# A sequence transform moved ahead of a gated MLP, with every MLP block in seven products

## The chip, the cores and the metric

The kernel runs on one core of one Trainium2 chip. The metric is device microseconds of one execution of the program. One execution on the chip is also profiled, and all rows below come from that one. Engines are named as the profile names them: PE (TensorE, matrix products; PEld is its weight load), DVE (VectorE), ACT (ScalarE), POOL (GpSimd) and SP (SyncE, which here only issues DMAs).

## The reference

`x` is 2048 tokens by 512 features. `xn` is its layernorm without affine terms. The first branch takes a discrete Fourier transform along the features and then along the tokens and keeps the real part. The second is an MLP with a sigmoid gate and 1792 hidden features. The output joins them.

```python
xn = (x - mean(x)) / sqrt(var(x) + 1e-5)
a, b = xn @ Wd_re.T, xn @ Wd_im.T            # 512 x 512 matrices
s = Ws_re @ a - Ws_im @ b                    # 2048 x 2048 matrices
h = sigmoid(xn @ w_gate) * (xn @ w_up)       # 512 x 1792 each
out = x + s * silu(h @ w_down)               # 1792 x 512
```

Both transforms are linear, so the sequence matrices can be applied to `xn` first and the feature matrices last. Both kernels do that.

## The kernel before

**Products.** Every value enters a product as two parts: `hi`, a copy rounded to fp32r that ACT writes, and `lo`, the rest, which DVE gets by a subtraction. `mm3` (lines 74 to 77) makes one product of three matmuls: hi by hi, hi by lo, lo by hi. A matmul has a weight of 128 by 128 and 512 moving columns, unless said otherwise. `Parts` makes the pair from a raw tile: one ACT instruction (line 71), then one DVE instruction (line 72).

**Seven products.** A block of two by two sub-blocks is multiplied by seven products in place of eight (Strassen's scheme in Winograd's form). The sums and differences that it needs are DVE instructions of `combine` (line 123). The products are numbered 1 to 7 and add up in chains "a", "b" and "c", each in two of the eight PSUM banks: ga and ua, gb and ub, gc and uc, or the two called pd. ACT snaps a chain's state between two products.

**Stages.** First the MLP: `BLOCKS` lists pairs (h, g), h being one of two halves of the tokens and g one of seven groups of 256 hidden features. Block (0, 0) is special (`start`, the local function `begin`): x arrives by tokens, is normalised on DVE, turned by 32 PE transposes (line 215), and multiplied in 192 matmuls of 256 columns (line 543) as the turned pieces come in. The other thirteen blocks compute gate and up by seven products (84 matmuls). Their down product is a `Seven` of 42 matmuls or, for group 2 in half 0, a `Plain` of 48; block (0, 0) has a `Ready` of 48. Each down product's result goes by `gather`: ACT evicts two banks into a page (line 309), POOL issues a DMA that adds the page onto `g_part` in DRAM (line 311). The second half's tokens are normalised while the first half's blocks run: DVE statistics, POOL arithmetic on the moments (lines 165 to 171), ACT normalisation (line 176), and a DMA of the result to `xn_part`. The same tokens are also needed as features by tokens; they are loaded so from `x_t` and normalised on DVE with moments broadcast from `m_part`.

Then the sequence transform (`seq_units`): four chunks of 512 output tokens, each 28 units of 12 matmuls. A unit is one product k for one pair of token blocks pp. Its weights are parts of normalised x, read back from `xn_part` and `s_part` and kept through all four chunks; its moving operand is a sum of blocks of the two cosine and sine matrices. Results and their sums go to `f_part`. Last the feature transform (`hidden_units`), 28 units of 12 matmuls, whose result is multiplied by silu of `g_part` (made ahead, stored in `gs_part`) and added onto the output by a DMA, the output having been filled with x.

**Order.** The kernel is recorded unit by unit, and each engine runs its instructions in the order recorded. For unit n the loop at the end of the kernel first runs what `sooner` put at n, then issues the loads of units n to n+5, then makes the parts of units n to n+2, then records the matmuls, then what `after` put at n. All buffers of SBUF are 54 pages of 4 KB per partition; a new page takes the place of one whose last use lies back, and the engine that writes it first waits for that use to end, a DMA's landing included. POOL's queue carries the moment arithmetic and the issues of all stores and adding DMAs; SP's carries all loads.

Of the kernel before, what the change touches and what calls it, by code (L numbers as in the profile page):

```python
# [36 lines left out]
def fnet_glu_kernel(ctx: ExitStack, tc: tile.TileContext, x, x_t, c_re, c_im, w_h, w_gu, w_down, out):  # L37
# [15 lines left out]
    ident = const.tile([P, P], F32, name="ident")  # L53
    make_identity(nc, ident)
    ones = const.tile([P, 512], F32R, name="ones")
    nc.vector.memset(ones.bitcast(F32), 1.0)
    mhalf = const.tile([P, 1], F32, name="mhalf")
    nc.gpsimd.memset(mhalf, -0.5)
    warm = const.tile([P, 1], F32, name="warm")
    nc.scalar.activation(warm, mhalf, AF.Sigmoid)  # L60
    moments = const.tile([P, 3, KH], F32, name="moments")
    m_part = dram.tile([2, 2, SB], F32, name="m_part")
    xn_part = dram.tile([2, 2, 2, P, 4, D // 2], F32, name="xn_part")
    g_part = [dram.tile([P, 2, SB], F32, name=f"g_part{i}") for i in range(2 * NT)]
    gs_part = dram.tile([2 * NT, P, 2, SB], F32, name="gs_part")
    f_part = dram.tile([NT // 2, 2, 7, P, 2, SB], F32, name="f_part")
    w_part = dram.tile([4, P, 4, D // 2], F32, name="w_part")
    s_part = dram.tile([2, 4, P, 4, D // 2], F32, name="s_part")
# [5 lines left out]
    def mm3(ps, ws, ms, first, last, go_on=False):  # L74
        nc.tensor.matmul(ps, ws[0], ms[0], start=first, stop=False, skip_group_check=go_on)  # L75
        nc.tensor.matmul(ps, ws[0], ms[1], start=False, stop=False, skip_group_check=go_on)  # L76
        nc.tensor.matmul(ps, ws[1], ms[0], start=False, stop=last, skip_group_check=go_on)  # L77
# [28 lines left out]
    class Parts(Value):  # L106


        def __init__(self, loads, src, shape, joint=False):
            def make():  # L110
                s = src()
                if joint:
                    both = page([2, *shape])
                    hi, lo = both[:, 0], both[:, 1]
                else:
                    hi, lo = page(shape), page(shape)
                split(hi, lo, s)
                return hi, lo

            super().__init__(loads, make)  # L120
# [5 lines left out]
    XK = {(0, 0): 1, (1, 0): 2, (0, 1): 0, (1, 1): 3}  # L126
    xop = {}
    xraw = {}
# [5 lines left out]
    extra, early = {}, {}  # L134
    now = [0]
# [6 lines left out]


    xs = {}

    def fetch(i, hold=False):
        pg = page([2, D], F32)
        if hold:
            nc.vector.memset(pg[:, 0, :1], 0.0)
        for j in range(2):  # L150
            xs[i + j] = pg[:, j, :]
            nc.sync.dma_start(xs[i + j], x[(i + j) * P : (i + j + 1) * P, :])

    st_of = {}

    def norm_a(i):
        st = stat.tile([P, 6], F32, name="st")
        mv = stat.tile([P, 2], F32, name="mv")
        rs = stat.tile([P, 2], F32, name="rs")
        nc.vector.bn_stats(st, xs[i])  # L160
        nc.vector.bn_aggr(mv, st)
        mean, scale = mv[:, 0:1], rs[:, 1:2]
        if i >= KH:
            mean, scale = (moments[:, m, i - KH : i - KH + 1] for m in range(2))
            nc.gpsimd.tensor_scalar(mean, mv[:, 0:1], 0.0, None, op0=ALU.add)
        nc.gpsimd.tensor_scalar(rs[:, 0:1], mv[:, 1:2], EPS, None, op0=ALU.add)
        nc.gpsimd.tensor_tensor(scale, rs[:, 0:1], mhalf, op=ALU.pow)
        if i >= KH:
            bias = moments[:, 2, i - KH : i - KH + 1]
            nc.gpsimd.tensor_tensor(bias, mean, scale, op=ALU.mult)  # L170
            nc.gpsimd.tensor_scalar(bias, bias, -1.0, None, op0=ALU.mult)
        st_of[i] = mean, scale

    def second_norm(i):
        scale, bias = (moments[:, m, i - KH : i - KH + 1] for m in (1, 2))
        nc.scalar.activation(xs[i], xs[i], AF.Identity, scale=scale, bias=bias)

    def norm_b(i):
        mean, scale = st_of.pop(i)
        nc.vector.tensor_scalar(xs[i], xs[i], mean, scale, op0=ALU.subtract, op1=ALU.mult)  # L180

    def turned_half(n, b, at):

        both = Load(m_part[b].rearrange("m t -> (m t)").partition_broadcast(P).rearrange("p (m t) -> p m t", m=2), [2, SB])
        raw = [Load(x_t[(2 + b) * 2 + j], [2, SB]) for j in range(2)]

        def store():
            at = slice(b * SB // P, (b + 1) * SB // P)
            for m in range(2):
                nc.gpsimd.dma_start(m_part[b, m].rearrange("(o p) -> p o", p=P), moments[:, m, at])  # L190

        def step(j, m):
            v = xraw[1, j, b] = raw[j].load()
            by = both.load()[:, m, :].unsqueeze(1).to_broadcast([P, 2, SB])
            nc.vector.tensor_tensor(v, v, by, op=(SUB, ALU.mult)[m])

        after(n, store)
        sooner(at[0] - 2, both.load)
        for i in range(4):
            if i % 2 == 0:  # L200
                sooner(at[i] - 4, raw[i // 2].load)
# [884 lines left out]
```

## Time and profile before

| | us |
|---|---|
| median of three runs | 813.24 |
| the three runs | 812.42, 813.24, 817.62 |
| span of the profiled execution | 809.7 |
| PE busy in it | 799.5 |
| DVE busy in it | 643.7 |
| ACT busy in it | 506.7 |
| POOL busy in it | 158.7 |
| moved by DMA | 191.00 MB |

The span runs from the first to the last instruction of the profiled execution; the runs are timed apart from it, so 3.5 us lie between its span and the median of the runs. Busy shares are to be read with care: matmuls overlap in the record (389 ns is the mean of one of 512 columns, but in a dense stretch one starts every 227 ns), so the time of a stretch is read from counts and windows and not from means.

### The profile page before, as it was taken

The numbers are of one execution on the slowest core, as the hardware profiler recorded it, in microseconds if no ns is written. First come the engines' busy times: TensorE is split into PE (matmuls) and PEld (weight loads), VectorE is DVE, ScalarE is ACT, GpSimd is POOL, SyncE is SP. The second block draws the span as 40 slices with busy tenths as digits, with TensorE's granted clock in tenths as the row PEclk, the third lists the DMA queues.
The fourth block names the chain that finished last, engine by engine and source line by source line (L and its number), as shares of the span: only waits on it lengthen the run. The fifth ranks groups of instructions, "written<-read, shape, count | busy, mean of one in ns | idle before, by whom it ended". The sixth has DMA issues, their size and how long they took to land.

```text
span 809.7 us, 10299 instructions
## 1 busy us (share of the span) xinstructions
PE 799.5 (99%) x3624; PEld 663.2 (82%) x3624; DVE 643.7 (80%) x807; ACT 506.7 (63%) x779; POOL 158.7 (20%) x237
## 2 busy tenths in 40 slices
PE   8999899999999999999999999999999999999997
PEld 7988788888888888888887888888888888888886
DVE  6898868976776778787787897888888876986945
ACT  4665868787677677778877774545445545546360
POOL 3156431221222222122121100011101110001201
PEclk9999999999999999999999999999999999999999
DMA  8456996977899997978999968278919994699986
GB/s 278 164 203 84 187 285 152 198 160 155 258 245 229 295 279 136 250 171 174 257 248 335 280 213 293 86 278 294 329 78 332 347 377 150 247 337 376 306 264 104
DMA packets 54931, 191.00 MB, mean 236 GB/s; under 512 B 6240, under 2 KB 6496, under 8 KB 54880
## 3 DMA queue, kind: packets, MB, share of 16 engines
q0 software_dynamic: 24480, 84.95, 46.3%
q1 hardware_dynamic: 30320, 105.33, 35.8%
q8 instruction: 28, 0.46, 0.2%
q14 instruction: 23, 0.19, 0.1%
q10 hardware_dynamic: 80, 0.07, 0.0%
HBM read 108.53 MB, written 85.47 MB: 240 GB/s over the span
## 4 chain that ended last, share of the span: by engine, by line
PE 91%; DMA 5%; DVE 1%; ACT 1%; issue 1%; POOL 1%; SPq 0%; ACTq 0%; DVEq 0%; POOLq 0%
PE pd L77 6%; PE pd L75 6%; PE pd L76 6%; PE ga L75 5%; PE ga L76 5%; PE ua L75 5%; PE ua L76 5%; PE ga L77 5%; PE ua L77 5%; PE gc L76 3%; PE gc L77 3%; PE gc L75 3%; PE uc L76 3%; PE uc L75 3%; PE uc L77 3%; PE ub L75 3%
## 5 line engine op out<-in xcount | busy, mean ns | idle before, releaser
L72 DVE TENSOR_TENSOR page<-page 128x1024 fp32r<-128x1024 f32 (+1 forms) x355 | 335.4, 974 | 105.7 <-ACT page L71 104.4
L71 ACT ACTIVATE page<-page 128x1024 fp32r<-128x1024 f32 (+1 forms) x355 | 287.7, 857 | 102.6 <-DVE page L123 81.4
L123 DVE TENSOR_TENSOR page<-page 128x1024 f32<-128x1024 f32 (+2 forms) x224 | 193.0, 881 | 1.5 <-DMA page<-in_w_gu_dram 0.8
L309 ACT ACTIVATE page<-pd 128x512 f32<-128x512 f32 x184 | 106.9, 597 | 50.7 <-PE pd L77 41.5
L311 POOL DMA_DIRECT2D g_part<-page x84 | 73.5, 958 | 283.2 <-ACT page L309 159.5
L75 PE MATMUL pd<-page 128*128 128x512 f32 x232 | 90.2, 389 | 0.0
L76 PE MATMUL pd<-page 128*128 128x512 f32 x232 | 90.2, 389 | 0.0
L77 PE MATMUL pd<-page 128*128 128x512 f32 x232 | 90.2, 389 | 0.0
L75 PE MATMUL ga<-page 128*128 128x512 f32 x200 | 78.3, 391 | 2.2 <-ACT page L462 2.2
L76 PE MATMUL ga<-page 128*128 128x512 f32 x200 | 77.9, 390 | 0.0
L77 PE MATMUL ga<-page 128*128 128x512 f32 x200 | 77.8, 389 | 0.0
L75 PE MATMUL ua<-page 128*128 128x512 f32 x200 | 77.8, 389 | 0.0
L76 PE MATMUL ua<-page 128*128 128x512 f32 x200 | 77.8, 389 | 0.0
L77 PE MATMUL ua<-page 128*128 128x512 f32 x200 | 77.8, 389 | 0.0
L76 PEld LDWEIGHTS pd<-page 128*128 128x128 f32 x232 | 43.5, 188 | 9.1
L77 PEld LDWEIGHTS pd<-page 128*128 128x128 f32 x232 | 43.5, 188 | 9.0
L75 PEld LDWEIGHTS pd<-page 128*128 128x128 f32 x232 | 43.5, 188 | 9.0
L76 PE MATMUL gc<-page 128*128 128x512 f32 x124 | 48.5, 391 | 0.3 <-DVE page L72 0.3
L75 PE MATMUL uc<-page 128*128 128x512 f32 x124 | 48.3, 389 | 0.0
L77 PE MATMUL gc<-page 128*128 128x512 f32 x124 | 48.3, 389 | 0.0
L76 PE MATMUL uc<-page 128*128 128x512 f32 x124 | 48.3, 389 | 0.0
L75 PE MATMUL gc<-page 128*128 128x512 f32 x124 | 48.3, 389 | 0.0
(134 smaller groups left out, 1305.5 us busy)
## 6 DMA issues: line engine op xcount, KB each, us to landing
g_part<-page POOLq DMA_DIRECT2D x92, 512.0 KB, 8.4
page<-f_part SPq DMA_DIRECT2D x36, 512.0 KB, 5.8
page<-in_c_re_dram SPq DMA_DIRECT2D x34, 512.0 KB, 6.6
page<-in_c_im_dram SPq DMA_DIRECT2D x33, 512.0 KB, 6.8
f_part<-page POOLq DMA_DIRECT2D x28, 512.0 KB, 6.7
page<-in_w_gu_dram SPq DMA_DIRECT2D x22, 512.0 KB, 6.5
page<-xn_part SPq DMA_DIRECT2D x14, 512.0 KB, 5.2
page<-in_w_down_dram SPq DMA_DIRECT2D x11, 512.0 KB, 8.6
```

The source lines that it names most:

```text
L71: nc.scalar.activation(hi, src, AF.Copy)
L72: nc.vector.tensor_tensor(lo, src, hi.bitcast(F32), op=SUB)
L75: nc.tensor.matmul(ps, ws[0], ms[0], start=first, stop=False, skip_group_check=go_on)
L76: nc.tensor.matmul(ps, ws[0], ms[1], start=False, stop=False, skip_group_check=go_on)
L77: nc.tensor.matmul(ps, ws[1], ms[0], start=False, stop=last, skip_group_check=go_on)
L123: (engine or nc.vector).tensor_tensor(dst, a, b, op=op)
L309: nc.scalar.activation(pg[:, o, :], po, AF.Copy, scale=float(sign))
L311: nc.gpsimd.dma_start(g_part[i], pg, accum_op=ADD)
```

## The change

The order of the stages is turned round. The sequence transform comes first. Chunks 0 and 1 run their products 1 and 2 interleaved, unit by unit, while x arrives: each pair of units shares one set of weights, a tile pair of x, normalised in place on ACT (half of the first pair on DVE) and split. Chunk 2's products 1 and 2 follow, then products 5, 6, 7, 3 and 4 of chunks 0, 1 and 2, then chunk 3. Sums of x are made in place on the resident tiles; `xn_part` and `s_part` are gone, and with them all PE transposes and matmuls of 256 columns at the head.

The MLP follows, on x as features by tokens from `x_t`, normalised on DVE with broadcast moments, for both halves now. All fourteen blocks, (0, 0) among them, are of seven products with a `Seven` down product; `start`, `Plain` and `Ready` are gone. The blocks of `f_raw` that the feature transform needs in sums are loaded again during the MLP, added on DVE and stored in `f_sum`. The last eight down products run between units of the feature transform's first pair. silu is made from `g_part` in place, with no trip through `gs_part`.

`Parts` is cut in three steps, so that for the next units all sums are recorded first, then all ACT copies, then all DVE subtractions. Some moments' arithmetic works on two columns at a time.

The matmuls change so: 3370 of 512 columns (10 of them idle ones for warming up), 222 of 256 and 32 transposes before; 3442 of 512 (10 idle) and 24 of 256 after.

**PE at the head, before.** PE's first rows: `ones` feeds the idle matmuls, `ident` the transposes into pd, and gb, ub are the banks of the first gate and up sums.

```order
L568 MATMUL gc<-ones 128x512 x10
L215 MATMUL pd<-ident,page 128x128 x4
L568 MATMUL gc<-ones 128x256 x2
L215 MATMUL pd<-ident,page 128x128 x4
L568 MATMUL gc<-ones 128x256 x4
L543 MATMUL gb<-page 128x256 x2
L543 MATMUL ub<-page 128x256 x2
```

**PE at the head, after.** The same place; ga, ua hold chunk 0's product 1 and gc, uc chunk 1's.

```order
L351 MATMUL gb<-ones 128x512 x4
L351 MATMUL ub<-ones 128x512 x4
L351 MATMUL pd<-ones 128x512 x2
L70 MATMUL ga<-page 128x512 x3
L70 MATMUL ua<-page 128x512 x3
L70 MATMUL ga<-page 128x512 x3
L70 MATMUL ua<-page 128x512 x3
L70 MATMUL gc<-page 128x512 x2
L70 MATMUL uc<-page 128x512 x2
```

The transposes and the half-width matmuls are gone; after ten idle matmuls PE goes straight to the sequence products.

**DVE at the head, before.** From the first statistics on (line 160): line 180 normalises a tile, 530 makes the lo part of a weight, 240 the lo part of turned x.

```order
L160 BN_STATS st_113<-page_108 128x6
L161 BN_AGGR mv_114<-st_113 128x2
L149 MEMSET page_120 128x1
L160 BN_STATS st_126<-page_108 128x6
L161 BN_AGGR mv_127<-st_126 128x2
L180 TENSOR_SCALAR page_108<-page_108,mv_114,rs_115 128x512
L180 TENSOR_SCALAR page_108<-page_108,mv_127,rs_128 128x512
L530 TENSOR_TENSOR page_133<-page_111,page_133 128x512
```

**DVE at the head, after.** From the statistics of the second tile pair (page_148) on: line 162 is the statistics, 123 the lo parts; page_190, 206, 246 and 264 are lo parts of sequence blocks for units 1 to 4, page_211 holds the parts of the second tile pair.

```order
L162 BN_STATS st_194<-page_148 128x6
L163 BN_AGGR mv_192<-st_194 128x2
L162 BN_STATS st_197<-page_148 128x6
L163 BN_AGGR mv_192<-st_197 128x2
L123 TENSOR_TENSOR page_190<-page_146,page_189 128x1024
L123 TENSOR_TENSOR page_206<-page_151,page_205 128x1024
L123 TENSOR_TENSOR page_211<-page_148,page_211 128x512
L162 BN_STATS st_216<-page_153 128x6
L163 BN_AGGR mv_214<-st_216 128x2
L162 BN_STATS st_219<-page_153 128x6
L163 BN_AGGR mv_214<-st_219 128x2
L123 TENSOR_TENSOR page_246<-page_156,page_245 128x1024
```

Statistics of a tile pair now stand between the lo parts that PE waits for, and no memset holds a load of x back.

**POOL in the MLP, before.** Around the first adding DMA onto `g_part` (line 311): lines 165 to 171 are the moments' arithmetic of a tile of the second half.

```order
L165 TENSOR_SCALAR moments<-mv 128x1
L166 TENSOR_SCALAR rs<-mv 128x1
L167 TENSOR_TENSOR moments<-rs,mhalf 128x1
L170 TENSOR_TENSOR moments<-moments 128x1
L171 TENSOR_SCALAR moments<-moments 128x1
L311 DMA g_part_83<-page 128x1024
L165 TENSOR_SCALAR moments<-mv 128x1
L166 TENSOR_SCALAR rs<-mv 128x1
```

**POOL in the MLP, after.** The densest place, in the block (1, 4) and the one after it: the issues of `g_part` alternate with stores of sums (`f_sum`) that wait for DVE.

```order
L653 DMA f_sum_104<-page 128x1024
L479 DMA g_part_83<-page 128x1024
L653 DMA f_sum_105<-page 128x1024
L479 DMA g_part_82<-page 128x1024
L653 DMA f_sum_106<-page 128x1024
L482 DMA g_part_84<-page 128x1024
L653 DMA f_sum_107<-page 128x1024
L479 DMA g_part_84<-page 128x1024
```

All moments' arithmetic has gone to the head of POOL's queue; what stands between the gathers now are stores.

The diff, cut to what the prediction speaks of:

```diff
-BLOCKS = ((0, 1), (0, 2), (0, 3), (0, 4), (1, 4), (1, 5), (0, 5), (0, 6), (1, 6), (1, 0), (1, 1), (1, 2), (1, 3))
-FIRST_TURNED = 1, 4
-SEVENS = 1, 3, 4, 5, 6
-LATE = 1, 4, 5, 6
+BLOCKS = ((0, 0), (0, 1), (0, 2), (0, 3), (0, 4), (1, 4), (1, 5), (0, 5), (0, 6), (1, 6), (1, 0), (1, 1), (1, 2), (1, 3))
...
+        def high(self):
+            if self.parts is None and self.at is None:
+                self.begin()
...
+                nc.scalar.activation(self.parts[0], self.raw, AF.Copy)
+
+        def make(self):
+            self.high()
+            hi, lo = self.parts
+            nc.vector.tensor_tensor(lo, self.raw, hi.bitcast(F32), op=SUB)
+            return hi, lo
...
+    def stats(j, pp):
...
+        for e in range(2):
+            st = stat.tile([P, 6], F32, name="st")
+            nc.vector.bn_stats(st, xs[j, pp][:, e, :])
+            nc.vector.bn_aggr(mv[:, e, :], st)
+        for at in each:
+            scale = moments[:, 1, pp, at, j]
+            nc.gpsimd.tensor_scalar(rs[:, at], mv[:, at, 1], EPS, None, op0=ALU.add)
+            nc.gpsimd.tensor_tensor(scale, rs[:, at], mhalf[:, at], op=ALU.pow)
+        mean, scale, bias = (moments[:, m, pp, :, j] for m in range(3))
+        nc.gpsimd.tensor_scalar(mean, mv[:, :, 0], -1.0, None, op0=ALU.mult)
+        nc.gpsimd.tensor_tensor(bias, mean, scale, op=ALU.mult)
+        return mv
+
+    def normalise(j, pp, es=(0, 1), d=None):
+        for e in es:
+            v = xs[j, pp][:, e, :] if d is None else a_block(d, j, pp)[:, e]
+            nc.scalar.activation(v, v, AF.Identity, scale=moments[:, 1, pp, e, j : j + 1], bias=moments[:, 2, pp, e, j : j + 1])
...
+        for i, k in enumerate((1, 2)):
+            for pp in range(4):
+                for c in chunks[:2]:
+                    add(c.needs(k, pp), lambda c=c, k=k, pp=pp: c.run(k, pp))
+                m = 8 * i + 2 * pp
+                if m > 4:
+                    sooner(m - 6, lambda i=i, pp=pp: fetch(i, pp))
+                if m > 2:
+                    sooner(m - 4, lambda i=i, pp=pp: stats(i, pp))
+                    sooner(m - 2, units[m][0][1].get)
+                    sooner(m - 2, lambda i=i, pp=pp: normalise(i, pp))
+                if i:
+                    after(m + 2, lambda pp=pp: store_moments(pp))
...
+    def f_sums(pair, half, at):
...
+        def step(i, dst, a, b):
+            nc.gpsimd.dma_start(f_sum[pair][half][i], combine(dst(), a.get(), b.get(), ADD))
...
-        job, begin = start(0, 0)
-        for i in range(KH):
-            after(i // 2, lambda i=i: store_xn(i))
-        last = None
+        chunks = begin_seq()
+        n = len(units)
+        x_norm(0, 0, (n - 36, n - 33, n - 30, n - 27))
+        x_norm(0, 1, (n - 24, n - 21, n - 18, n - 15))
+        x_ops(0, (n - 12, n - 10, n - 9, n - 7, n - 6, n - 4, n - 3, n - 2, n - 1, n - 0, n + 2))
+        last, job = None, None
...
-            job = block(h, w, made, job, Seven(h, wd, made) if h or g in SEVENS else Plain(h, g), g in LATE)
+            job = block(h, w, made, job, Seven(h, wd, made))
+        x_norm(1, 0, (n + 9, n + 12, n + 15, n + 18))
+        x_norm(1, 1, (n + 21, n + 22, n + 24, n + 25))
+        x_ops(1, (n + 27, n + 28, n + 29, n + 30, n + 31, n + 32, n + 33, n + 34, n + 35, n + 36, n + 38))
+        for p in range(2):
+            for half in range(2):
+                f_sums(p, half, n + 40 + 12 * (2 * p + half))
+        w_sums(n + 84)
...
+            ahead = [p for _, (ps, _) in zip(range(SPLIT_AHEAD + 1), units[n:]) for p in ps]
+            for p in ahead:
+                p.begin()
+            for p in ahead:
+                p.high()
+            for p in ahead:
+                p.get()
```

In `x_norm` and `x_ops` n is the MLP's first unit. A half needs eight DVE instructions of 1024 elements to normalise it, four for its sums and seven for its lo parts.

More of the change, by code (lines that the diff above doesn't have):

```diff
@@ L72, in split, with mm3 @@
         nc.vector.tensor_tensor(lo, src, hi.bitcast(F32), op=SUB)
[L74 to L77, printed above, removed]
+    def mm3(ps, ws, ms, first, last, go_on=False, late=False, only=(0, 1, 2)):
+        pairs = ((0, 0), (1, 0), (0, 1)) if late else ((0, 0), (0, 1), (1, 0))
+        for i in only:
+            w, m = pairs[i]
+            nc.tensor.matmul(ps, ws[w], ms[m], start=first and i == 0, stop=last and i == 2, skip_group_check=go_on)
     class Load:
@@ L174, in second_norm, with amid @@
[L174 to L190, printed above, removed]
+    def amid(n, f):
+        middle.setdefault(n, []).append(f)
@@ L449, in run, with block @@
             gather(self.first + 2 * b + i, self.ps, sign)
-    def block(h, w, made, before, job, late):
+    def block(h, w, made, before, job):
         s, ps = job.s, {}
@@ L976, in hidden_units @@
                 if k in BLOCK:
[L977 removed]
+                    g, sigmoid, times = silu(pair, *BLOCK[k])
+                    at = n - 24 + 7 * (2, 4, 7, 3).index(k) if pair == 0 else m - 2
+                    sooner(at - 4, g.load)
+                    after(at - 1, sigmoid)
+                    after(at, times)
                 if (pair, k) == LAST:
[L979 removed]
+                    sooner(m - 4, xlast.load)
                     add([hp[k, 0], hp[k, 1], w[k]], run_last)
```

818 lines of the change are left out of this document (308 added, 510 removed).

## The prediction

> **What bounds the kernel now.** I read the page's first lines and its chain of waits first, then the waits of PE alone, then windows cut at the stages.
>
> ```profile
> span 809.7 us, 10299 instructions
> PE 799.5 (99%) x3624; PEld 663.2 (82%) x3624; DVE 643.7 (80%) x807; ACT 506.7 (63%) x779; POOL 158.7 (20%) x237
> PE 91%; DMA 5%; DVE 1%; ACT 1%; issue 1%; POOL 1%; SPq 0%; ACTq 0%; DVEq 0%; POOLq 0%
> ```
>
> PE is busy nearly all the time, and the chain runs along it. The windows (PE, PEld, DVE, ACT, POOL busy, each with its count, then PE's clock, the DMA engines' busy share and GB/s) tell where it isn't dense.
>
> ```profile
> 0.00:8.10 8.10, 5.92 (x24) 4.43 (x24) 4.27 (x10) 3.08 (x7) 2.43 (x11) 1.00 0.64 205
> 8.10:35.40 27.30, 26.94 (x217) 25.90 (x217) 22.15 (x51) 15.40 (x42) 7.49 (x14) 1.00 0.68 248
> 35.40:66.00 30.60, 30.58 (x136) 25.00 (x135) 27.42 (x42) 19.67 (x33) 16.30 (x31) 1.00 0.44 155
> 66.00:90.00 24.00, 21.81 (x95) 17.40 (x94) 20.73 (x34) 17.05 (x32) 15.60 (x28) 1.00 1.04 180
> 90.00:400.00 310.00, 310.00 (x1368) 256.42 (x1367) 240.16 (x361) 234.28 (x411) 70.73 (x87) 1.00 0.91 212
> 400.00:440.00 40.00, 39.68 (x174) 32.20 (x173) 30.95 (x34) 30.75 (x46) 7.52 (x9) 1.00 0.97 278
> 803.10:809.70 6.60, 1.47 (x13) 1.26 (x11) 2.23 (x4) 0.00 (x0) 0.00 (x0) 0.76 0.75 139
> ```
>
> From 90 to 400 us PE never waits and starts a matmul every 310/1368 = 0.2266 us. That is the price of a matmul of 512 columns here; the time is their number times it, plus the head, a few waits and a tail of 6.6 us. From the timeline of PE, the first half-width matmul and the first of full width, and from the chain at the end a half-width one:
>
> ```profile
> 8.12 0.51 PE L543 MATMUL gb<-page 128*128 128x256 f32 x2
> 35.42 0.40 PE L75 MATMUL ga<-page 128*128 128x512 f32 x1
> 799.91 0.12 PE gb L77
> ```
>
> From 35.42 to 803.1 lie 767.7 us. In them are 3360 full products (3370 less the 10 idle ones), 761.4 us; 24 half-width ones at 0.12, 2.9 us; the two holes of the windows (2.2 and 0.3), 2.5 us; 0.9 is left over. So the sum reproduces the body. The hole of 2.2 us, in the chain between 66 and 90 us:
>
> ```profile
> 76.31 0.24 POOL moments L171
> 76.79 9.84 DMA g_part<-page
> 86.73 0.61 ACT page L462
> 87.38 0.50 PE ga L75
> ```
>
> POOL issued the adding DMA only after moments that had waited for DVE; the page that it read came free late, ACT's snap waited for the page, and PE for the snap.
>
> **The change, part by part.** *Matmuls.* By the counts, full products go from 3360 to 3432: block (0, 0) had 192 of half width and a down product of 48, and now has 84 + 42; the down product of (0, 2) goes from 48 to 42. So +72 × 0.2266 = +16.3 us. The 192 half-width ones and the 32 transposes go, and all of them lay before 35.42.
>
> *The head.* Let T0 be the start of a gap-free stream of products. Before, the full products began at 35.42. After, they begin once x and a block of the cosine matrix are in and split. The rows for that: arrival of the first tile and of the third load, a tile's statistics, an ACT normalisation, a copy, the rate of SP's loads (MB, share of 16 engines' span), and the moments' arithmetic on POOL from its first to its fourth instruction, once quick and once slow.
>
> ```profile
> 3.46 0.69 DVE L160 BATCH_NORM_STATS2 st<-page 128x6 f32<-128x512 f32 x1 [2.07 <-DMA page<-in_x_dram]
> 6.19 0.63 ACT L526 ACTIVATE page<-page 128x512 fp32r<-128x512 f32 x1 [3.97 <-DMA page<-in_w_gu_dram]
> L160 DVE BATCH_NORM_STATS2 st<-page 128x6 f32<-128x512 f32 x16 | 10.9, 682 | 2.2 <-DMA page<-in_x_dram 2.1
> L161 DVE BATCH_NORM_AGGREGATE mv<-st 128x2 f32<-128x6 f32 x16 | 2.9, 182 | 0.8
> L176 ACT ACTIVATE page<-page,moments 128x512 f32<-128x512 f32 x8 | 6.0, 808 | 0.0
> q1 hardware_dynamic: 30320, 105.33, 35.8%
> 71.24 0.21 POOL L165 TENSOR_SCALAR moments<-mv 128x1 f32<-128x1 f32 x1 [3.91 <-DVE mv L161]
> 72.45 0.19 POOL L170 TENSOR_TENSOR moments<-moments 128x1 f32<-128x1 f32 x1
> 73.25 0.61 POOL L165 TENSOR_SCALAR moments<-mv 128x1 f32<-128x1 f32 x1
> 76.03 0.19 POOL L170 TENSOR_TENSOR moments<-moments 128x1 f32<-128x1 f32 x1
> ```
>
> By 6.19 the first 1.05 MB had landed (two x tiles and half a megabyte of weights). After, the second pair of x tiles ends 2.1 MB; the second 1.05 MB takes 2.9 us at 105.33 MB / (0.358 × 809.7) = 363 GB/s, so it lands at 9.1. Statistics 2 × 0.86 make it 10.8; POOL's four instructions take 1.4 (71.24 to 72.64) or 3.0 (73.25 to 76.22), so 12.2 to 13.8; two normalisations and a copy, 1.6 + 0.6, so 14.4 to 16.0 for the first matmul of unit 2. Two units of 12 lie ahead of it, 5.4 us: T0 is 9.0 to 10.6. Then DVE is next, in the order shown: a lo part, two statistics pairs around two lo parts of full size, one more lo part. For these I need starts of DVE that follow each other without a wait:
>
> ```profile
> 501.38 1.23 DVE L72 TENSOR_TENSOR page<-page 128x1024 fp32r<-128x1024 f32 x1 [4.95 <-ACT page L71]
> 502.52 1.22 DVE L123 TENSOR_TENSOR page<-page 128x1024 f32<-128x1024 f32 x1
> 200.63 1.29 DVE L72 TENSOR_TENSOR page<-page 128x512 fp32r<-128x512 f32 x2 [2.22 <-ACT page L71]
> L123 DVE TENSOR_TENSOR page<-page 128x256 f32<-128x256 f32 x36 | 14.4, 421 | 0.3
> ```
>
> So 1.14 us for 1024 elements, 0.60 for 512, 0.42 for 256. From 14.4 to 16.0: 0.6 + 1.7 + 2.3 + 1.7 + 0.6 = 6.9, so 21.3 to 22.9 for the third matmul of unit 4, which comes 50 matmuls (11.3 us) into the stream: T0 is 10.0 to 11.6. From there DVE has 4.6 us of work per pair of units against PE's 5.4, and catches up. I take 10.5. Bounds: 8.1, where before got its first product out of the same first tile, and 14, if the x pair is later by another landing of 3.4 us, the median of the x tiles' issues to landing:
>
> ```profile
> page<-in_x_dram SPq DMA_DIRECT2D x16, 256.0 KB, 3.4
> ```
>
> [...]
>
> *The second half's moments* leave the MLP, and POOL's queue with them; the hole of 2.2 us goes, and nothing in that place is next. That of 0.3 lay on a load of `s_part`, which goes as well.
>
> *DVE in the MLP.* A block with new weights has 30 DVE instructions of 512, 4 of 256 and 2 of 1024: 18.0 + 1.7 + 2.3 = 22.0 us beside 126 × 0.2266 = 28.6 of PE. Into units n+21 to n+38 (18 units of 4.08 us, 73.4) fall 15 instructions of 1024 for the second half's x, 17.1 us, and 18/7 of a block, 56.6: 73.7 us, all of the time. The densest stretch before, 35.4 to 66, had DVE at 27.42 of 30.60, 90%, and PE did not wait. The cover is that parts are made two units, 8.2 us, ahead. The cost is 0 if that holds and 73.7/0.9 − 73.4 = 8.5 if DVE can't go above 90%. I take 1, nearer to the row in which PE ran on.
>
> *Loads and pages.* `xn_part`, `s_part` and `gs_part` go, `f_raw` is loaded again for the sums; what hides these is DMA that is not full past 440:
>
> ```profile
> 440.00:700.00 260.00, 260.00 (x1148) 214.96 (x1147) 218.79 (x199) 138.88 (x162) 24.76 (x41) 1.00 0.73 253
> ```
>
> silu for the last pair is now made three units after its load; a load that lands late holds ACT. 0 to 4 us, taken as 1, from the window 400 to 440, where 0.3 was lost at a DMA share of 0.97.
>
> *Sum.* Span = 10.5 + 777.7 (3432 × 0.2266) + 2.9 + 0.9 + 6.6 + 2 = 800.6, against 809.7: −9.1. The profiled span lies 3.5 below the median of 813.24, so 804.1 us, a gain of 1.1%.
>
> **The rivals.** *Pages run out in the MLP* (slower). While both halves are in use, their parts hold 28 of the 54 pages, a block's weights 11, its down weight 6, its values 4: five are left. Three new pages per unit make a gather's page come round after some two units, 8.2 us. The rows of eviction, issue and landing:
>
> ```profile
> L309 ACT ACTIVATE page<-pd 128x512 f32<-128x512 f32 x184 | 106.9, 597 | 50.7 <-PE pd L77 41.5 <-issue 3.6 <-ACT page L71 0.3
> g_part<-page POOLq DMA_DIRECT2D x92, 512.0 KB, 8.4
> ```
>
> Two evictions 1.2, an issue of about 1 and 8.4 are 10.6, 2.4 too late. From n+38 to the end of the first half at n+62 that is 12 times 2.4, 29 us in place of the 2 taken, so 831. It decides for slower than before from 0.4 us per unit (9.1/24) on. Against it: before held the same 28 pages and ran 310 us without a wait. For it: stores of sums and their loads now come on top, in bursts of four units, 4.2 MB in 16.3 us beside the gathers, where before the DMA engines were at 0.91 with 212 GB/s.
>
> *DVE or the head takes the gain* (no change to tell): 8.5 in place of 1 for DVE, T0 at 14: 804.1 + 7.5 + 3.5 = 815. The row of 90% speaks for it, the cover of two units against.
>
> *All goes well*: T0 8.1 and no wait, 804.1 − 2.4 − 2 = 799.7.
>
> That the change does not do what it says is excluded for PE by the counts.
>
> **How the numbers follow.** A measurement of this kernel can tell about 1%, 8.1 us: faster is below 805.1, slower above 821.4. The forecast has 0.45, all goes well 0.15, the second rival 0.30, pages 0.10. The forecast's own range is 801 to 808, and three quarters of it with the good case lie below 805.1, some 0.48; the second rival's lower end adds 0.07: faster 0.55. Slower is the page case above half its price, 0.08; the rest, 0.37, is the same. The range from 798 to 816 leaves out most of the page case and the ends.
>
> **What the profile after would show.** Right: matmuls of `ga` dense from 10 to 12 us on, PE's busy share 98% or 99% with a span near 801, no PE wait in the sequence stage past 30 us. The head is wrong if PE idles past 25 us. DVE as the bound would show as PE waiting for lo parts about 410 to 440 us, with DVE above 95% there; pages as ACT waiting for `g_part` DMAs between 470 and 560 us, and PE for ACT. The forecast would be wrong by its base if a matmul's 0.2266 does not hold in the new order.

## The result, and the profile after

The changed kernel takes 834.73 us (median of four runs, 830.84 to 839.99) against 812.92 for the kernel before: a ratio of 1.0264, 95% interval 1.0222 to 1.0306. It is slower, where 804 was forecast, and it lies outside the range of 798 to 816. The profiled execution has a span of 829.1 us, 28.5 above the sum of 800.6.

The head of the page after: the span, the busy time of each engine, the shares of the chain.

```profile
span 829.1 us, 9918 instructions
PE 799.4 (96%) x3466; PEld 651.0 (79%) x3466; DVE 668.1 (81%) x851; ACT 523.6 (63%) x802; POOL 141.9 (17%) x195
PE 58%; DMA 24%; DVE 6%; issue 5%; POOL 3%; ACT 3%; SPq 0%; POOLq 0%; DVEq 0%; ACTq 0%
```

The chain, 91% PE before, is now 58% PE and 24% DMA. PE's busy time tells little here, because a matmul at half the granted clock counts as busy (from 8.20 to 11.70 us PE is busy for all of the 3.50 us, with 9 matmuls at a clock of 0.51); the numbers of matmuls in windows tell more. The windows after, cut at the places where time is lost (columns as in the prediction):

```profile
0.00:36.00 36.00, 30.25 (x105) 22.67 (x106) 23.75 (x42) 20.59 (x29) 14.24 (x29) 0.91 0.96 373
36.00:112.00 76.00, 71.90 (x308) 56.64 (x307) 63.62 (x75) 47.11 (x64) 14.30 (x22) 1.00 0.54 121
112.00:470.00 358.00, 358.00 (x1581) 296.21 (x1580) 316.96 (x371) 214.81 (x310) 35.64 (x49) 1.00 0.64 185
470.00:640.00 170.00, 168.71 (x743) 138.91 (x742) 124.01 (x184) 121.78 (x218) 41.66 (x55) 1.00 0.96 245
640.00:740.00 100.00, 92.31 (x391) 73.59 (x390) 82.25 (x120) 73.92 (x128) 19.98 (x26) 0.98 1.01 284
740.00:780.00 40.00, 38.36 (x165) 30.49 (x165) 27.63 (x29) 28.10 (x39) 10.87 (x12) 1.00 1.05 287
780.00:829.10 49.10, 39.90 (x184) 32.47 (x182) 29.84 (x34) 17.28 (x20) 5.21 (x5) 0.95 0.89 234
```

The time lost in a window is its length less its matmuls at 0.2266 us. The 10 idle products of the first window don't count, and the last window holds the 24 half-width ones at 0.12. (A matmul that crosses a bound counts in both windows, so each is up to 0.4 us short, and a dense window comes out at -0.3.) This gives 14.5, 6.2, -0.3, 1.6, 11.4, 2.6 and 10.0 us.

- The price of a matmul held: 358 us in a row go at 0.2266, the whole of the sequence transform past 112 us and the first third of the MLP.
- The head cost 14.5 against the 10.5 taken, and then 6.2 more came before 112 us.
- The largest part is lost between 640 and 740 us, in the last quarter of the MLP and at the start of the feature transform, where the forecast had nothing.

Which wait ends last there? First the hole at 651 us: the timeline of PE, and ACT's waits between 640 and 660 us.

```profile
655.48 1.85 PE L70 MATMUL ga<-page 128*128 128x512 f32 x6 [3.65 <-ACT page L583]
ACT page L583 <- DMA f_sum<-page: 4.5, 1, 4.5
```

PE waits for a snap of ACT, and ACT for a page whose store of a sum had not landed. By the trace it is the store issued at 638.63 us, which landed at 654.74. POOL's timeline shows why it was late:

```profile
611.96 0.84 POOL L479 DMA_DIRECT2D g_part<-page  x1 [3.22 <-ACT page L477]
624.77 2.60 POOL L479 DMA_DIRECT2D g_part<-page  x3 [11.97 <-ACT page L598]
628.28 0.84 POOL L479 DMA_DIRECT2D g_part<-page  x1 [0.92 <-ACT page L477]
636.26 0.85 POOL L479 DMA_DIRECT2D g_part<-page  x1 [7.13 <-ACT page L477]
636.80 0.87 POOL L653 DMA_DIRECT2D f_sum<-page  x1
637.43 1.11 POOL L479 DMA_DIRECT2D g_part<-page  x1
638.63 0.57 POOL L653 DMA_DIRECT2D f_sum<-page  x1
640.86 0.88 POOL L479 DMA_DIRECT2D g_part<-page  x1 [1.66 <-ACT page L477]
642.17 0.56 POOL L653 DMA_DIRECT2D f_sum<-page  x1 [0.43 <-DVE page L127]
658.97 0.85 POOL L479 DMA_DIRECT2D g_part<-page  x1 [16.24 <-DMA g_part<-page]
659.52 0.86 POOL L653 DMA_DIRECT2D f_sum<-page  x1
660.06 2.06 POOL L479 DMA_DIRECT2D g_part<-page  x2
```

Down products 2 and 1 follow each other by one unit, 4.08 us, and add onto the same tile of `g_part`; 7 and 5 do so two units apart. POOL stands at the later add until the earlier one has landed. The add of 611.96 landed at 624.26, and half a microsecond later POOL went on, after a wait of 11.97 us (the row names an ACT instruction that ended about then). It issued three adds at once, then a fourth, and stood 7.13 us until one of the three had landed, at 635.76. Then six DMAs went out within six microseconds, three adds and three stores of sums. They landed one after another, from 644.73 to 660.49, and the store that ACT needed was the fourth. The wait of 16.24 us behind them, for the add of 640.86, begins after that store was issued: it is not what made it late, but it makes the next burst.

The sums of POOL's waits given below are those that the profile puts down to a landing. Waits like those of 11.97 and 7.13 us end behind a landing too, but are not in them.

In the kernel before, POOL's timeline has the same shape, and PE lost nothing there:

```profile
306.43 2.61 POOL L311 DMA_DIRECT2D g_part<-page  x3 [11.36 <-ACT page L309]
318.89 2.61 POOL L311 DMA_DIRECT2D g_part<-page  x3 [9.85 <-ACT page L309]
```

So bursts were there already; new is how much shares the queue and the DMA engines with them. It is not simply that stores stand among the adds: at 290 us in the kernel before, behind a wait of 10.38 us, two stores of `s_part` did so too, with the DMA engines at 1.01 and 276 GB/s from 284 to 300 us, and PE ran on. Around the hole, from 636 to 655 us, the changed kernel has 1.05 and 323 GB/s.

### The profile page after: what moved, and what is told of

It is laid out like the page before. It is cut to its first block, busy times and chain, and to the rows that moved or that the text cites. A ratio compares the mean times of both kernels' runs of the same rounds, so it can differ in the third digit from the quotient of the medians.

```text
span 829.1 us, 9918 instructions
## 1 busy us (share of the span) xinstructions
PE 799.4 (96%) x3466; PEld 651.0 (79%) x3466; DVE 668.1 (81%) x851; ACT 523.6 (63%) x802; POOL 141.9 (17%) x195
## 4 chain that ended last, share of the span: by engine, by line
PE 58%; DMA 24%; DVE 6%; issue 5%; POOL 3%; ACT 3%; SPq 0%; POOLq 0%; DVEq 0%; ACTq 0%
DMA g_part<-page 16%; PE pd L70 14%; PE ga L70 11%; PE ua L70 11%; PE uc L70 7%; PE gc L70 7%; PE gb L70 4%; PE ub L70 4%; DMA page<-in_c_im_dram 3%; DVE page L123 3%; DMA page<-g_part 2%; DMA out_dram<-page 2%; ACT page L118 2%; POOL g_part L479 1%; DVE page L127 1%
## 5 line engine op out<-in xcount | busy, mean ns | idle before, releaser
L123 DVE TENSOR_TENSOR page<-page 128x512 fp32r<-128x512 f32 (+1 forms) x384 | 349.8, 939 | 92.3 <-ACT page L118 85.9
L118 ACT ACTIVATE page<-page 128x512 fp32r<-128x512 f32 (+1 forms) x384 | 303.5, 831 | 146.3 <-DVE page L127 106.7
L70 PE MATMUL pd<-page 128*128 128x512 f32 (+1 forms) x984 | 241.2, 388 | 8.8 <-DVE page L123 4.5
L70 PE MATMUL ga<-page 128*128 128x512 f32 x600 | 156.5, 395 | 9.1 <-ACT page L583 4.0
L70 PE MATMUL ua<-page 128*128 128x512 f32 x600 | 155.7, 395 | 0.0
L70 PEld LDWEIGHTS ga<-page 128*128 128x128 f32 x600 | 111.9, 189 | 37.8 <-ACT page L583 5.0
L70 PEld LDWEIGHTS ua<-page 128*128 128x128 f32 x600 | 115.0, 192 | 24.3
L70 PEld LDWEIGHTS gc<-page 128*128 128x128 f32 x384 | 72.4, 189 | 15.2
L70 PEld LDWEIGHTS uc<-page 128*128 128x128 f32 x384 | 72.1, 188 | 15.0
L70 PE MATMUL gb<-page 128*128 128x512 f32 x252 | 65.7, 393 | 3.1 <-DVE page L123 2.9
## 6 DMA issues: line engine op xcount, KB each, us to landing
page<-f_sum SPq DMA_DIRECT2D x16, 512.0 KB, 14.4
```

Of the source, the lines that this page charges most:

```text
L70: nc.tensor.matmul(ps, ws[w], ms[m], start=first and i == 0, stop=last and i == 2, skip_group_check=go_on)
L118: nc.scalar.activation(self.parts[0], self.raw, AF.Copy)
L123: nc.vector.tensor_tensor(lo, self.raw, hi.bitcast(F32), op=SUB)
```

## The experiments

Three theories stood for the loss after 470 us. **A**: the wait for the same tile makes bursts, and pages come late. **B**: the DMA engines simply have too much to move there. **C**: too few pages, the prediction's own rival. For the 20 us before 112 us, the head's chain and the stores of moments were tried. The losses below are worked out from windows with the same bounds as above.

### The order of the down products

```diff
-    SEVEN = (2, 1, 6, 7, 4, 5, 3)
+    SEVEN = (1, 6, 7, 4, 2, 5, 3)
```

> The changed kernel with the seven products of a down block in the order 1, 6, 7, 4, 2, 5, 3 in place of 2, 1, 6, 7, 4, 5, 3, so that two adds onto the same g_part tile lie at least three units apart in place of one. Theory A (POOL stands in its queue until an earlier add onto the same tile has landed, and then issues three or four DMAs at once, whose pages come late): POOL's waits for landings of g_part, 51.5 us in the changed kernel, fall below 20, PE's lost time between 640 and 776 us, 14.7 us, falls below 5, and the median falls from 834.7 to 822 to 828. Theory B (the DMA engines have too much to move there): POOL's waits change their name, PE loses 12 to 17 us as before, 831 to 838. Theory C (too few pages): as B.

Measured: 834.9 us, as slow as the changed kernel. But the 11.4 us between 640 and 740 us became 1.4 (435 matmuls in 100 us), and POOL's waits for landings of `g_part` fell from 51.5 to 21.4 us, the longest from 16.2 to 5.8. The time came back elsewhere: 5.2 us between 112 and 470 (1557 matmuls), of which three waits for gathers' evictions make 2.5, and 9.6 between 740 and 780 (134). A holds for the place, not for the total, and the edit was not clean: it moved DVE's and ACT's work too. Why evictions came late before 470 us stays open.

### The sums further apart

```diff
-            after(at + i, lambda i=i, v=v: step(i, *v))
+            after(at + 3 * i, lambda i=i, v=v: step(i, *v))
```

> The changed kernel with the sums of the transformed tiles and of the feature matrix made and stored one every three units in place of one every unit. Theory A (POOL behind the same tile's add): the bursts are a part of the trigger only; 3 to 8 of the 14.7 us go, 826 to 832. Theory B (DMA engines overloaded by bursts of stores and loads beside the gathers): the holes at 651 us and at 692 to 719 us (8.6 us together) go and nothing new comes, 822 to 827. Theory C (too few pages): raw tiles live longer, the loss grows, 835 to 842.

The same edit was made to the loads, and to the sums of the feature matrix. Measured: 832.66 us, between the numbers of A and of C, with 11.2 lost between 640 and 740 us. Moving the same bytes more evenly saved nothing, which speaks against B in the form that a burst of stores by itself is to blame.

### A tile of its own for product 2

```diff
+    g_two = [dram.tile([P, 2, SB], F32, name=f"g_two{h}") for h in range(2)]
...
-            gather(self.first + 2 * b + i, self.ps, sign)
+            gather(-1 - self.first // 4 if k == 2 else self.first + 2 * b + i, self.ps, sign)
```

> The changed kernel with the down product 2 gathered onto a tile of its own for each half, which nothing reads: the output lacks that product's share; all counts and bytes stay, and the order of the products too. Two adds onto one tile now lie at least two units apart. Theory A (POOL waits for the landing of an add onto the same tile, then issues a burst): POOL's waits for landings of g_part fall from 51.5 to below 20 us, the time that PE loses between 640 and 740 us, 11.8 us, falls below 5, the median from 834.7 to 822 to 828. Theory B (too much for the DMA engines): the loss stays, 831 to 838.

Measured: 823.34 us, in a kernel that leaves product 2's share out of its output. Windows of it between 470 and 780 us, and POOL's timeline at the place shown above:

```profile
470.00:640.00 170.00, 169.93 (x750) 140.37 (x749) 125.25 (x186) 124.15 (x219) 41.70 (x56) 1.00 0.99 257
640.00:740.00 100.00, 99.79 (x440) 82.25 (x439) 87.13 (x125) 84.36 (x142) 24.28 (x31) 1.00 1.05 293
740.00:780.00 40.00, 33.49 (x128) 25.51 (x127) 25.50 (x27) 17.96 (x23) 7.45 (x7) 0.91 1.06 306
```

```profile
635.31 0.85 POOL L481 DMA_DIRECT2D g_part<-page  x1 [2.68 <-ACT page L478]
637.10 0.57 POOL L655 DMA_DIRECT2D f_sum<-page  x1 [0.93 <-DVE page L128]
639.49 0.86 POOL L481 DMA_DIRECT2D g_two<-page  x1 [1.82 <-ACT page L478]
640.64 0.56 POOL L655 DMA_DIRECT2D f_sum<-page  x1 [0.29 <-DVE page L128]
643.07 0.87 POOL L481 DMA_DIRECT2D g_part<-page  x1 [1.88 <-ACT page L478]
```

The gathers now go one by one, every 4 us, with the sums between them. 440 matmuls fit into the 100 us from 640 on, a loss of 0.3 in place of 11.4, while the DMA engines' share is even higher, 1.05 with 293 GB/s. So A explains the loss in the MLP, and B doesn't by itself. POOL's waits for `g_part` landings were to fall below 20 us and fell from 51.5 to 22.2. But 11.0 us are lost from 740 to 780, where 2.6 were: PE waits there for copies by ACT, and these for loads of `w_part` and of the feature matrix, which landed 16 to 26 us after their issue. From 470 us to the end, without the tail of 6.6, 10.7 us are lost in place of 19.0, so part of what the MLP gains goes in the last stage. There B is not excluded.

### Products 2 and 1 in one DMA

```diff
+        if keep:
+            return pg
+        if other is not None:
+            combine(pg, pg, other, ADD)
...
-            gather(self.first + 2 * b + i, self.ps, sign)
+            other = self.two if k == 1 else None
+            self.two = gather(self.first + 2 * b + i, self.ps, sign, other, keep=k == 2)
```

> The changed kernel with the results of down products 2 and 1 added on DVE, page onto page, and gathered by one DMA in place of two: 14 adding DMAs fewer, 14 DVE instructions of 1.14 us more. Theory A (same tile): as the kernel with a tile of its own, 820 to 828. Theory B (DMA engines): 7.3 of the 77.6 MB of POOL's queue go, half of the loss after 470 us at most, 825 to 831. If DVE is what bounds the MLP, its 16 us more show as PE waiting for lo parts between 400 and 560 us, 836 to 850.

Measured: 820.18 us, within A's numbers. From 640 to 740 us 2.1 us are lost and from 740 to 780 none (178 matmuls in 40 us): with 14 adds fewer PE is dense in the last stage too, although the DMA engines' share is still 1.06 there. 2.2 us are lost between 112 and 470, 1.8 of them in two waits for a snap that ACT makes behind a copy that waited for DVE. So the additions on DVE are not free.

### The sums made in place

```diff
+                t1 = Value([a0, a1], onto(a0.load, a1.load))
+                t2 = Value([b1], onto(t1.get, b1.load))
+                t3 = Value([b1], onto(a1.load, b1.load))
+                t4 = Value([b0], onto(t2.get, b0.load))
...
-                f_sums(p, half, n + 40 + 12 * (2 * p + half))
```

> The changed kernel with the sums for the feature transform made from the four raw tiles where they are used, in place, as the sequence transform does: 16 stores of sums and 28 loads of half a megabyte go, DVE's 16 additions move into the last stage. Theory A (same tile): the burst at 651 us loses its stores and the loss there (5.5 us) shrinks to 0 to 3, the rest between 680 and 740 stays: 828 to 833. Theory B (DMA engines, in the last stage above all): the loss from 740 us to the end, 5.8 us and 2 us of tail, falls below 3, the burst goes too: 818 to 826. Rival: DVE holds PE in the last stage, 834 to 845.

Measured: 819.53 us. The adds onto the same tile stand here as in the changed kernel; 16 stores of sums and 28 loads of half a megabyte are gone. The windows between 470 and 780 us:

```profile
470.00:640.00 170.00, 170.00 (x752) 140.76 (x751) 110.03 (x174) 124.01 (x218) 34.32 (x42) 1.00 0.85 179
640.00:740.00 100.00, 98.54 (x434) 80.96 (x433) 88.27 (x128) 82.71 (x139) 21.63 (x27) 1.00 1.01 263
740.00:780.00 40.00, 37.69 (x158) 30.09 (x157) 35.30 (x36) 22.92 (x30) 10.02 (x10) 0.96 1.01 261
```

1.7 us are lost from 640 to 740 and 4.2 from 740 to 780, and the time lies in B's numbers; but for the MLP B alone is excluded by the run with a tile of its own, where no byte was taken away. POOL still stands: by the trace eight waits of 6 to 11 us between 640 and 780 us end half a microsecond behind a landing, where the changed kernel has seven of 10 to 16. So these waits cost PE little alone, as in the kernel before; together with the stores and loads of the sums 11 us are lost. Either one taken away, the loss between 640 and 740 us goes. It was an expectation of neither theory by itself. Whether the stores count here by their places in POOL's queue or, with the loads, by their bytes is not separated: this edit takes both away.

### Three pages fewer

```diff
-PAGES = 54
+PAGES = 51
```

> The changed kernel with 51 pages in place of 54. Theory C (pages run out while both halves' x is held, 470 to 553 us, as the prediction's rival had it): the loss between 470 and 560 us, 2.0 us, grows to over 8 us, 842 to 860. Theory A (pages only come late while POOL stands): it grows by 0 to 4 us there, 834 to 841.

Measured: 853.45 us. The two windows past 470 us:

```profile
470.00:640.00 170.00, 157.60 (x667) 127.98 (x667) 108.22 (x159) 104.25 (x187) 37.00 (x49) 0.97 0.90 226
640.00:740.00 100.00, 93.69 (x399) 75.39 (x399) 83.19 (x125) 74.69 (x132) 22.48 (x29) 0.98 1.04 271
```

Between 470 and 640 us, 18.9 us are lost in place of 1.6, 17.5 of them before 560 us, where C had put them; between 640 and 740, 9.6 in place of 11.4. The rival of pages is real and three pages away, but it sits in another place than the changed kernel's loss. What is lost past 640 us does not grow with fewer pages; whether more pages would shrink it is not shown.

### The head: statistics earlier, moments later, and both

```diff
+        stats(0, 2)
         normalise(0, 1)
...
-                    sooner(m - 4, lambda i=i, pp=pp: stats(i, pp))
+                    if m > 4:
+                        sooner(m - 5, lambda i=i, pp=pp: stats(i, pp))
```

> The changed kernel with the statistics of each pair of x tiles put ahead of the lo parts that wait for the pair before, on DVE. Theory A (the head is a ring: a lo part on DVE, the next pair's statistics behind it, POOL's moments of 3.3 us, ACT's normalisation, the next lo part): unit 4, which starts at 24.9 us, starts at 20 to 22, the time lost before 36 us falls from 14.6 to 11 to 13, the median by 2 to 4 us to 831 to 833. Theory B (the head goes at the rate of the loads of x and of the cosine matrix): no change before 36 us, 833 to 837.

Measured: 836.22 us. Unit 4 started at 24.8 us, as in the changed kernel; the loss up to 36 us fell only from 14.5 to 13.8. What did go are the waits at 42 and 49 us, in the second round of tiles. PE does not wait ahead of unit 4 any more, but gets there no sooner: it runs two windows at half its clock on the way (last section), with a mean clock of 0.91 up to 36 us, and the 24 matmuls from 17.29 us up to unit 4 take 7.47 us, where 0.2266 each would make 5.44. The last run below has the same head and shows one such window, 0.95 up to 36 us, and there unit 4 started at 23.1 us. Between 36 and 112 us 8.0 us are lost (300 matmuls) in place of 6.2, in holes from 76 to 91 us; the first of them waits for a load of the cosine matrix that took 25 us to land. That can't be put down to this edit: the five kernels above the one with fewer pages have the changed kernel's head, and lost 14.5 to 16.5 us up to 36 us and 6.4 to 10.3 from there to 112.

```diff
-                    after(m + 2, lambda pp=pp: store_moments(pp))
+                    after(30 + 10 * pp, lambda pp=pp: store_moments(pp))
```

> The changed kernel with the eight stores of moments after units 30, 40, 50 and 60 in place of units 10, 12, 14 and 16. Theory A (their many small packets hold up the loads of the sine matrix, one of which took 25.8 us): loads issued between 55 and 66 us land within 13 us, the hole of 2.9 us at 88 us goes, none of more than 1 us takes its place later, where loads are fewer: 830 to 833. Theory B (eleven loads and two stores of half a megabyte in a row are late by their own number): the hole stays, 833 to 837. It may also come again near a store of moments: then the loss moves and the time stays.

Measured: 832.33 us. DMA issues between 55 and 70 us with their median from issue to landing, of the changed kernel and then of this one:

```profile
page<-in_c_im_dram SPq DMA_DIRECT2D x5, 512.0 KB, 20.7
m_part<-moments POOLq DMA_DIRECT2D x4, 2.0 KB, 23.1
```

```profile
page<-in_c_im_dram SPq DMA_DIRECT2D x7, 512.0 KB, 4.9
```

Eight stores of 2 KB held the loads of half a megabyte at 20.7 us; without them beside, these take 4.9. The hole is gone (326 matmuls from 36 to 112 us, a loss of 2.1 in place of 6.2), and where the stores stand now, nothing is lost.

> The changed kernel with the statistics a step earlier and the stores of moments later, both together. Alone, the one saved about 3 us before 60 us and lost them again at the late sine matrix, the other saved 4.3 us before 112 us. Theory A (two separate costs): the time lost up to 112 us falls from 21.2 to 13 to 15, and the median by as much, to 826 to 829. Rival (what is gained early is lost again, since the stage after 470 us goes by its DMAs and not by PE): the loss up to 112 us falls so, but the median stays at 831 to 835.

Both together: 828.33 us, and PE is dense from 36 us on, by this kernel's window:

```profile
36.00:112.00 76.00, 76.00 (x337) 62.94 (x336) 68.51 (x79) 51.28 (x69) 6.63 (x9) 1.00 0.38 134
```

The two costs are separate from each other, and 6.4 us of the gain reach the median. Not all of it does in the profiled execution: there 7.5 us less are lost up to 112 us, but 24.0 in place of 19.0 from 470 us on, 15.9 of them between 640 and 740.

### All together

> Four edits together: statistics a step earlier, stores of moments later, products 2 and 1 gathered by one DMA, the sums of the feature transform made in place. If the four costs are separate, the time lost up to 112 us falls from 21.2 to 13 to 15, the loss from 470 us to the last product from 19.6 to 3 to 6, and the median from 834.7 to 805 to 811, at or below the 813 of the kernel before. If what is saved at one place is lost at the next (the last stage going by its DMAs), 815 to 822.

Measured: 812.32 us, ratio 0.9983 (0.9970 to 0.9996), a little above the 805 to 811 expected of separate costs. Up to 112 us 13.7 are lost and from 470 us on 6.0, both as expected. Here 2.2 us are lost between 112 and 470, as with the merge alone.

> The same without the one DMA for products 2 and 1, so the adds onto the same tile stand as in the changed kernel, but without stores of sums beside them. If the wait for the same tile costs only together with the stores (as the run with sums in place says: 2 us between 470 and 740 us), 806 to 813, near the kernel with all four. If it costs by itself, 5 to 10 us more than that one.

Measured: 810.13 us, ratio 0.9955 (0.9939 to 0.9971): the fastest of all, 24.6 below the changed kernel and 0.3 to 0.6% below the one before. Once the sums are gone the merge does not pay: with it the kernel took 2.2 us more. What is left, by its windows:

```profile
470.00:640.00 170.00, 170.00 (x752) 140.77 (x751) 111.00 (x176) 124.50 (x220) 34.55 (x42) 1.00 0.87 185
640.00:740.00 100.00, 96.78 (x414) 79.14 (x413) 84.81 (x117) 79.98 (x134) 21.59 (x28) 0.97 1.00 254
```

The 6.2 us past 640 lie at 714 to 724, where the feature transform begins: PE waits 3.2 us there for lo parts from DVE, which is busy all of these ten microseconds, and the granted clock is 0.70 on average. They were tried with the feature matrix's sums made in place too:

```diff
+        v1 = Value([a21, a22], lambda: combine(page([4, D // 2], F32), a21.load(), a22.load(), SUB))
+        v3 = Value([a11, a21], third)
+        v2 = Value([a11], second)
+        v4 = Value([a12], lambda: combine(a12.load(), a12.load(), v2.get(), ADD))
...
-        w_sums(n + 84)
```

> The kernel without the merge, and with the feature matrix's sums made in place from its four raw tiles too, at the start of the last stage: 4 stores and 7 loads of half a megabyte fewer between 660 and 730 us. Theory A (at the end of the MLP an add that waits for its tile lets a burst through, and the burst lands late because of the stores and loads beside it): the loss of 6.3 us at 714 to 724 falls to 0 to 3, median 803 to 808. Rival (DVE holds PE there: five instructions of 1.14 us more in that place, since the additions now lie where the stage begins): the loss stays or grows, 810 to 815.

Measured: 818.47 us, ratio 1.0059 (1.0039 to 1.0079). The loss between 640 and 740 us did not fall, but came to 7.5 us (408 matmuls), with a DMA share of 0.94. The fall that A expected did not come, and the rival was right in this, though the time lies above its 815: PE waits for lo parts from DVE at 712, 718 and 726 us, where the additions now lie. The 8.3 us more in the median are not explained by it; the profiled execution, 814.57 us, was the fastest of eight.

## Why the prediction was wrong

*The matmuls* were right: 3432 full products at 0.2266, and nothing lost from 112 to 470 us.

*DVE in the MLP* was right: taken at 1 us. In the place that the forecast named, DVE is at 95% and PE does not wait, so parts two units ahead were cover enough:

```profile
400.00:440.00 40.00, 40.00 (x178) 33.13 (x177) 37.93 (x56) 33.24 (x58) 8.29 (x10) 1.00 0.86 160
```

*Loads and pages* is the step that failed, and it carries most of the miss. It read "what hides these is DMA that is not full past 440" and took 1 us. Measured were 1.6 from 470 to 640, 11.4 to 740, 2.6 to 780, and 3.4 beyond the tail of 6.6 at the end, some 19 in all, 17 more than the 2 taken for DVE and these, of the 28.5 that the sum was short. Two things were overlooked.

- The window of the kernel before that stood for the cover, 440 to 700 at 0.73, had five of the 92 gathers in it; the changed kernel has 60 of its 98 there. POOL's queue, half of whose bytes are adds, took more of the engines per byte than SP's: before, it had 84.95 MB at 46.3% of the span, 227 GB/s, SP's 105.33 MB at 35.8%, 363 GB/s. In the changed kernel's burst at 691 us the stores landed 1.2 and 1.3 us behind the DMA ahead of them, the adds 2.6 to 3.8. A share read in one stage can't be taken for a stage that gets other traffic.
- The stores of sums were costed as bytes, not as places in POOL's queue, which already stood for an add's landing, 51.6 us in all in the kernel before and 51.5 after. The two runs that took away one side each, the wait, or the stores with their loads, show that the 11.4 us need both. From how much traffic on they do is open, since the kernel before had both at 290 us and lost nothing.

*The rival of pages* came to 831, nearly the profiled time. That is a coincidence, for it had another reason and another place: it put 29 us between units n+38 and n+62, where 1.6 were lost. With three pages fewer it comes true, 18.9 us.

*The head* was undersized: 14.5 against 10.5, though above the bound of 14 only by a little. What failed is the chain from unit 2 to unit 4. Unit 2 began at 16.91 us, against 14.4 to 16.0: POOL's four instructions ahead of it took 3.3 us, where the slow case had 3.0. From there on the forecast counted DVE's work alone, 6.9 us up to the third matmul of unit 4. But the next pair of tiles goes through statistics, POOL, ACT's normalisation and copy once more, one after the other, and unit 4 began at 24.87, 8.0 us behind unit 2. And DVE did not catch up, as the forecast had it: PE waited at 42 us and 49 us too, in waits that go when the statistics are put earlier. The two windows at half clock of the last section lie in these 14.5 us but do not set them: the run with the sums further apart has the same head and shows one, with a mean clock of 0.95 up to 36 us in place of 0.91, and its unit 4 began at 25.3 us, after 0.8 us of waiting; the run with the other order has a clock of 1.00 there, and lost 15.2 us up to 36 us. The slow case of POOL's moments did come. These are POOL's first two moment instructions of two pairs, in the timeline after:

```profile
19.28 1.12 POOL L166 TENSOR_SCALAR rs<-mv 128x2 f32<-128x2 f32 x1 [4.64 <-DVE mv L163]
20.48 1.54 POOL L167 TENSOR_TENSOR moments<-rs,mhalf 128x2 f32<-128x2 f32 x1
...
23.16 0.22 POOL L166 TENSOR_SCALAR rs<-mv 128x2 f32<-128x2 f32 x1 [0.56 <-DVE mv L163]
23.46 0.71 POOL L167 TENSOR_TENSOR moments<-rs,mhalf 128x2 f32<-128x2 f32 x1
```

The first pair ran beside lo parts on DVE (two, 2.34 us from 19.11 on), the second while DVE waited (1.78 us, up to 24.85): 2.7 against 1.0 us.

*The second half's moments*: "the hole of 2.2 us goes, and nothing in that place is next". The hole went, but the moments' stores went to a new place with it, beside the first loads of the sine matrix, and cost 4.1 us there (6.2 less 2.1, by one execution of each). The step counted what was removed from POOL's queue and not what was put beside other loads.

## What to carry to other kernels

When work moves, follow each queue that it is moved into: what waits there already, and what shares the DMA engines at that place. An idle share read before the change is no cover for traffic that the change itself brings along. In an in-order queue, two DMAs that add onto one target a unit apart turned a steady stream into bursts here; PE lost nothing by them in the kernel before, and 11 us when stores and loads that it needed in time came on top.

## What the runs showed of the hardware

A wait of PE can cost more than its length. Two windows of the changed kernel, before the hole at 651 us and just behind it:

```profile
643.80:647.20 3.40, 3.40 (x17) 2.81 (x16) 3.40 (x6) 3.19 (x7) 0.00 (x0) 1.00 1.01 381
655.60:659.50 3.90, 3.90 (x12) 3.11 (x13) 3.83 (x6) 3.33 (x7) 0.53 (x1) 0.65 0.83 294
```

Behind it the granted clock is 0.65 on average and 12 matmuls take 3.9 us, which is 1.2 us more than at 0.2266. In the head it happens twice:

```profile
8.20:11.70 3.50, 3.50 (x9) 2.76 (x9) 3.36 (x8) 1.98 (x3) 1.34 (x4) 0.51 1.05 416
18.50:21.90 3.40, 3.40 (x10) 2.64 (x9) 3.37 (x5) 0.25 (x1) 2.54 (x2) 0.50 1.03 416
```

9 and 10 matmuls in place of some 15 each, together worth 2.6 us. Each of these three stretches at half clock lasted 3.41 us by the trace: from 8.25 to 11.66 us, from 18.49 to 21.90 and from 656.78 to 660.19. A wait of 1.83 us, at 15 us, went ahead of the second, while the hole of 2.8 us at 88 us left the clock at 1.00. In the run with the other order 6.4 us were lost from 36 to 112 us, where the changed kernel lost 6.2, but at a mean clock of 0.98, some 3 us at half by that, in place of 1.00. So the length of a wait alone does not tell what it costs.

Small stores were dear for others here: eight of 2 KB each, on POOL's queue, took the median landing of half a megabyte on SP's queue from 4.9 to 20.7 us.
